# Re-ordering a one-core layer kernel: a scheduler with measured durations, weight norms on other engines, and one row sent ahead

## The chip, the cores and the metric

The kernel runs on one core of a Trainium2 chip. The metric is the device time of one execution in microseconds (us); the medians below come from three to seven executions. The executions of this study were spread over several chips, so a kernel is compared with the kernel before of the same call wherever that can be done. A ratio is the mean time of one kernel's fast runs over that of the other's fast runs in the same rounds, so it is not quite the ratio of the medians quoted. For one core, a run is called slow when it lies over 1.5% above the fastest run of the same kernel. A "pause" of PE is the time from the start of one matmul to the start of the next, less the time that such a matmul usually takes (0.216 us for 512 columns).

Names: PE is TensorE, PEld its weight loads, DVE is VectorE, ACT is ScalarE, POOL is GpSimd, SP is SyncE, which issues most transfers.

## The reference, cut to what matters

```python
def _A_ref(x, wqkv, w_phi, wo):        # H = 32 heads of 16
    ...                                # q, k, v = x @ wqkv
    phi_q = concat(softmax(q @ w_phi), softmax(-(q @ w_phi)));  phi_k likewise
    kv = phi_k^T v;  z = sum(phi_k);  o = (phi_q kv) / (phi_q z + 1e-6)
    return o @ wo
def _B_ref(x, w_gate, w_up, w_down):   # D = 512, F = 1792
    return ((x @ w_gate) * (x @ w_up)) @ w_down
xn = layernorm(x)                      # 2048 tokens x 512
return x + _A_ref(xn, ...) + _B_ref(xn, ...)
```

## The kernel before

The program is a list of steps, each with an engine, its reads and its writes. A scheduler written in Python turns the list into one fixed order per engine before the kernel is built; semaphores are then placed from the reads and writes. The order on PE is given by the program ("pinned"); the other engines' orders come from the scheduler's model of time. On the chip each engine runs its list strictly in order (below, DVE stands 4.58 us before one instruction while the next ones wait).

The main loop walks 19 slots `t`. A slot does the k features of token tile `t`, two or three "up units" (gate and up matmuls of 128 rows of F for 512 tokens, then a gate multiply on DVE that frees their PSUM banks, the `ps` tiles that matmuls write), v, from slot 8 on q features, and pieces of side work: norms of the weights (to choose power-of-two scales for half precision), scaling of the weights by DVE, sums and differences of weight blocks ("combinations", used for a multiplication with seven instead of eight products), and, for the first 512 tokens, whose inputs were centred but not divided by their standard deviation, a multiply of h by a row of r2 = 1/variance ("normalise", on POOL).

```python
def row_of_r2():                       # slot 10: after the scale sh of h is known
    pool(lambda e: e.tensor_scalar(out=r2s, in0=r2, scalar1=sh, ...), ["r2", "sh"], ["r2s"], 4)
    row = nc.dram_tensor("r2row", (ND, 128), F32, kind="Internal").ap()
    o = row.rearrange("t p -> p t")    # 128 partitions x 4 values: 512 writes of 4 bytes
    sc.dma(SP, lambda e: e.dma_start(o, r2s, allow_slow_non_contiguous=True), ["r2s"], ["r2row"], 131072)
    ...                                # read back, spread over all partitions
    sc.dma(SP, lambda e: e.dma_start(r2w, wide), ["r2row"], ["r2w"] + ks, 262144, free=ks)

def scales(t):                         # side work of slot t
    if t in (9, 10):   ...             # squares of wv, wo on ACT
    if 2 <= t < 9:                     # squares of w_gate and w_up on ACT, one each per slot
        squares("wg", t - 2, last); squares("wu", t - 2, last)
    elif t == 10:
        h_scale(); row_of_r2()
    if 7 <= t < 10:    wd_moments(...)     # 14 bn_stats of w_down on DVE
    if t == 11:        d_scale()
    if 12 <= t < 15:   scale_weights(todo[3 * (t - 12):3 * (t - 11)], last)
    elif t == 16:      combine_weights(1); combine_weights(2)
    elif t == 17:      combine_weights(3)
    ...
# in slot t:
    if 10 <= t < NT + 1:
        normalise(range(2 * (t - 10), 2 * (t - 9)), [("hT", *latest[0])])

def _order(sc):                        # the scheduler
    LAT, DMA_ISSUE, DMA_FIXED, TURN_ISSUE = 200.0, 550.0, 1700.0, 1300.0
    ...                                # of the ready steps of an engine, that with the best
                                       # priority among those that can start within 100 ns
```

Of the kernel before, what the change touches and what calls it, by code (L numbers as in the profile page):

```python
# [125 lines left out]
def _build(nc, es, A_x, A_wqkv, A_w_phi, A_wo, B_w_gate, B_w_up, B_w_down, out):  # L126
# [246 lines left out]
    def w_fold(w, dt, b=None):  # L373
        b = misc_bank() if b is None else b

        def fn(e):
            ins = None
            for jt in range(NQ):
                ins = e.matmul(bank(b, jt * 128, 128), lhsT=wT_v[:, w, jt, dt * 128:(dt + 1) * 128],  # L379
                               rhs=wbd_v[:, jt, :], start=True, stop=True)  # L380
            return ins
        sc.step(PE, fn, [("wT", w, jt) for jt in range(NQ)] + [("wbd", jt) for jt in range(NQ)], [("ps", b)], 4 * 60.0)
        if w == 1 or dt % 2 == 0:
            act(Wp_v[:, w, dt, :], bank(b), [("ps", b)], [("Wp", w, dt)])
        else:
            dve(lambda e: e.tensor_copy(out=Wp_v[:, w, dt, :], in_=bank(b)), [("ps", b)], [("Wp", w, dt)], 512)
# [264 lines left out]
    def squares(src, i, after):  # L651
        j = squared[0] % 4
        squared[0] += 1
        junk = hT_v[:, NF - 8 + 2 * j:NF - 6 + 2 * j, 3 * 512:4 * 512]
        over = [("junk", j)] if squared[0] > 4 else []
        if src in ("wv", "wo"):
            v, col, key = (wv_v, 14 + i, [("wv", i)]) if src == "wv" else (wo_v, 16 + i, ["wo"])
            act(junk, v[:, 2 * i:2 * i + 2, :], key + after + over, [("junk", j), ("ssq", col)], func=ACTF.Square,
                accum=ssq[:, col:col + 1])
        else:  # L660
            v, col = (wg_v, i) if src == "wg" else (wu_v, 7 + i)
            i_ap = v[:, :, i * 256:(i + 1) * 256].rearrange("p (a b) c -> p a b c", a=2)
            key = [(src, k) for k, (lo, n) in enumerate(SLICES) if lo < (i + 1) * 256 and lo + n > i * 256]
            act(junk.rearrange("p a (b c) -> p a b c", b=2), i_ap, key + after + over, [("junk", j), ("ssq", col)],
                func=ACTF.Square, accum=ssq[:, col:col + 1])
# [4 lines left out]
    def wd_moments(fts, after):  # L670
        sc.prio = 2
        for ft in fts:
            dve(lambda e, ft=ft: e.bn_stats(wst[:, ft, :], wd_v[:, ft, :]), ["wd"] + after, [("wst", ft)], 512)  # L673
        sc.prio = 1
        if fts[-1] == NF - 1:
            dve(lambda e: e.bn_aggr(wmv, sbf("wst", 0, NF * 6)), [("wst", ft) for ft in range(NF)], ["wmv"], 84)
            dve(lambda e: e.scalar_tensor_tensor(out=wmv[:, 0:1], in0=wmv[:, 0:1], scalar=wmv[:, 0:1], in1=wmv[:, 1:2],
                                                 op0=ALU.mult, op1=ALU.add), ["wmv"], ["wms"], 1)
            dve(lambda e: e.tensor_scalar(out=ssq[:, 18:19], in0=wmv[:, 0:1], scalar1=NF * 512.0, scalar2=None,
                                          op0=ALU.mult), ["wms"], [("ssq", 18)], 1)  # L680
# [11 lines left out]

    def norms(lo, groups, c0):
        n, k = sum(groups), len(groups)
        cols = [("ssq", c) for c in range(lo, lo + n)]
        dve(lambda e: e.tensor_copy(out=ssqb[:, lo:lo + n], in_=ssq[:, lo:lo + n]), cols, [("ssqb", lo)], n)
        b = misc_bank()
        mm(bank(b, 0, n), [(nc.const_aps.tensor(1.0, (128, 128), BF16), ssqb[:, lo:lo + n])], [("ssqb", lo)], b)
        for i, m in enumerate(groups):
            at = sum(groups[:i])  # L700
            dve(lambda e, i=i, m=m, at=at: e.tensor_reduce(out=scl[:, c0 + i:c0 + i + 1], in_=bank(b, at, m),
                                                           axis=AX.X, op=ALU.add), [("ps", b)], [("nrm", lo, i)], m)
        act(scl[:, c0 + 4:c0 + 4 + k], scl[:, c0:c0 + k], [("nrm", lo, i) for i in range(k)] + ["eps"], [("lnn", lo)],
            func=ACTF.Ln, bias=tiny)
        act(scl[:, c0 + 8:c0 + 8 + k], scl[:, c0 + 4:c0 + 4 + k], [("lnn", lo)], [("rn", lo)], func=ACTF.Exp,
            scale=-0.5)

    def h_scale():
        norms(0, (7, 7), 8)
        dve(lambda e: e.tensor_tensor(out=scl[:, 20:21], in0=scl[:, 16:17], in1=scl[:, 17:18], op=ALU.mult),  # L710
            [("rn", 0)], ["rgu"], 1)
        power_of_two(sh, scl[:, 20:21], ["rgu"], "sh", 8.0)


    def d_scale():
        norms(14, (2, 2, 1), 24)
# [29 lines left out]
    def row_of_r2():  # L746
        pool(lambda e: e.tensor_scalar(out=r2s, in0=r2, scalar1=sh, scalar2=None, op0=ALU.mult), ["r2", "sh"], ["r2s"],
             4)
        row = nc.dram_tensor("r2row", (ND, 128), F32, kind="Internal").ap()
        o = row.rearrange("t p -> p t")  # L750
        sc.dma(SP, lambda e: e.dma_start(o, r2s, allow_slow_non_contiguous=True), ["r2s"], ["r2row"], 131072)
        ks = [("x", 12), ("x", 13)]
        wide = bass.AP(tensor=row.tensor, offset=row.offset, ap=[[0, 128], [1, ND * 128]])
        sc.dma(SP, lambda e: e.dma_start(r2w, wide), ["r2row"], ["r2w"] + ks, 262144, free=ks)

    def normalise(fts, after):
        sc.prio = 2
        for ft in fts:
            pool(lambda e, ft=ft: e.tensor_tensor(out=hH_v[:, ft, 0:512], in0=hT_v[:, ft, 0:512], in1=r2w,  # L759
                                                  op=ALU.mult), [("hT", ft, 0), "r2w", ("x", 12), ("x", 13)] + after,  # L760
                 [("hT", ft, 0)], 512)
        sc.prio = 1

    r2s = scl[:, 4:4 + ND]
    r2w = sbf("x", 3072, 512)
# [12 lines left out]
    def combine_weights(k):  # L778
# [3 lines left out]
        for name, t, blk, n, src, ov in (("tw", tw, wd_block, NK, [("wdh", i) for i in range(7)], over),  # L782
                                         ("two", two, wo_block, 2, [("woh", i) for i in range(2)], ov_o)):
            i0, i1 = {1: (blk(0, 1), blk(0, 0)), 2: (blk(1, 1), t[1]), 3: (blk(1, 1), blk(0, 1)),
# [58 lines left out]
    glu = [0]  # L843
    raw = set()
# [24 lines left out]
    def gate(ft, sg, bg, bu, s):  # L869
        g = sb("g", s * 512, 512)  # L870
        if "sh" not in sc.writer:
# [180 lines left out]
    def scales(t):  # L1052
        last = [("hT", *latest[0])] if latest[0] else []
        if t in (9, 10):
            for i in range(2):
                squares("wv" if t == 9 else "wo", i, last)
        if 2 <= t < 9:
            squares("wg", t - 2, last)
            squares("wu", t - 2, last)
        elif t == 10:  # L1060
            h_scale()
            row_of_r2()
        if 7 <= t < 10:
            wd_moments(((0, 1, 2, 3, 4, 5), (6, 7, 8, 9), (10, 11, 12, 13))[t - 7], last)
        if t == 11:
            d_scale()
        if 12 <= t < 15:
            scale_weights(todo[3 * (t - 12):3 * (t - 11)], last)
        elif t == 16:
            combine_weights(1)  # L1070
            combine_weights(2)
        elif t == 17:
            combine_weights(3)
        if t == 11:
            halves.extend([to_half(1), to_half(2)])
        if t >= 11:
            half_step(1)
# [26 lines left out]
    for t in range(NT + 3):  # L1104
# [9 lines left out]
        x_next(t + 4)  # L1114
        late_loads(t)
# [6 lines left out]
        if 12 <= t < NT + 1:  # L1122
            if t not in (14, 16):
                up()
            if t in (13, 15):
                q_next()
# [5 lines left out]
        else:  # L1132
            up()
            if 8 <= t < NT + 1:
                q_next()
            if 10 <= t < NT + 1:
                normalise(range(2 * (t - 10), 2 * (t - 9)), [("hT", *latest[0])])
            if 3 <= t < NT + 2:
                kv_acc(t - 3)
            if t < 12 and t != 10:  # L1140
                up()
        if 4 < t < 8:
            w_fold(0, (0, 1, 3)[t - 5])
    h_combine(0)
# [32 lines left out]

def _order(sc):


    LAT, DMA_ISSUE, DMA_FIXED, TURN_ISSUE = 200.0, 550.0, 1700.0, 1300.0
    dma_free = 0.0
    steps = sc.steps
    remaining = [len(st.deps) for st in steps]
# [11 lines left out]
    free_at = {e: 0.0 for e in ready}  # L1196
    new_order = {e: [] for e in ready}
    order = []
    while len(order) < len(steps):
        best = None  # L1200
        for e, lst in ready.items():
            if pos[e] < len(fixed[e]):
                lst = [p for p in lst if not steps[p[1]].pin or p[1] == fixed[e][pos[e]]]
            if lst:
                fa = free_at[e]
                soon = min(max(p[0], fa) for p in lst) + 100.0
                cand = min((p for p in lst if p[0] <= soon), key=lambda p: (steps[p[1]].prio, max(p[0], fa), p[1]))
                key = (max(cand[0], fa), cand[1])
# [7 lines left out]
        if isinstance(st.lane, tuple):  # L1216
            issue = TURN_ISSUE if st.turn else DMA_ISSUE
            free_at[e] = start + issue
            dma_free = max(dma_free, start + issue) + st.cost
            st.finish = dma_free + DMA_FIXED  # L1220
        else:
            free_at[e] = start + st.cost
            st.finish = free_at[e]
# [3 lines left out]
        for d in dependents[idx]:  # L1227
            remaining[d.idx] -= 1
            ready_time[d.idx] = max(ready_time[d.idx], st.finish + (LAT if d.lane != st.lane else 50.0))
# [86 lines left out]
```

## Time and profile before

| | before |
|---|---|
| time, three runs | 215.57, 215.76, 216.53 us |
| the run that was profiled | 219.02 us, span 217.3 us |
| PE busy | 96% |
| matmul pauses from 108 to 141 us | 4.0 us |

The page of the kernel before, busy time of the engines and two rows of the 40 slices (each digit is a tenth of a slice of 5.4 us):

```profile
PE 209.5 (96%) x1476; PEld 124.9 (57%) x1476; DVE 174.4 (80%) x279; ACT 145.2 (67%) x349; POOL 114.3 (53%) x138
PE   7899999999999999999999998699999999999995
PEclk9999999999999999999999999999999999999999
PE 80%; DVE 12%; issue 3%; DMA 3%; ACT 1%; SPq 0%
```

The last line is the chain of work that ended last, by engine: mostly PE, with DVE for 12%. The "86" in the PE row, at 130 to 141 us, is where PE was short of work. The list of waits of PE names the releaser (engine, tile, line; then total us, times, longest us):

```profile
PE ps L247 <- DVE arena L878: 3.0, 3, 1.7
PE ps L985 <- PEq L1301: 0.8, 1, 0.8
```

L878 is the gate multiply on DVE. In the same trace the groups of DVE instructions by shape (busy us, mean ns) and two transfers in the list of DMAs (KB each, median us from issue to landing) read:

```profile
L733 DVE TENSOR_SCALAR arena<-arena 128x1024 f16<-128x1024 bf16 x9 | 7.8, 899 | 0.1
L787 DVE TENSOR_TENSOR arena<-arena 128x1792 f16<-128x1792 f16 x4 | 7.7, 1914 | 0.0
arena<-in_A_x_dram SPq DMA_DIRECT2D x3, 512.0 KB, 4.3
r2row<-arena SPq DMA_DIRECT2D x1, 2.0 KB, 8.2
```

Weight scaling (L733) and combinations (L787) are the DVE instructions that meet POOL at the port the two share.

### The profile page before, as it was taken

What the parts mean: (1) busy time and instruction counts of PE and PEld (TensorE: products, weight loads), DVE (VectorE), ACT (ScalarE), POOL (GpSimd) and SP (SyncE); (2) the same over time, 40 slices, a digit from 0 to 9 for tenths busy, and PEclk for the clock granted to TensorE, in tenths of its full rate; (3) what the DMA queues carried; (4) which work ended last, traced back from release to release, by engine and by line L of the source; (5) the groups of instructions that cost most, each with busy time, mean ns of one, the idle gap of its engine ahead of it and who ended that gap; (6) DMA issues with size and microseconds to landing.
All of it is one profiled execution on the core that took longest, in us unless ns stands there. A gap on an engine that the chain in (4) does not pass through costs nothing.

```text
span 217.3 us, 4042 instructions
## 1 busy us (share of the span) xinstructions
PE 209.5 (96%) x1476; PEld 124.9 (57%) x1476; DVE 174.4 (80%) x279; ACT 145.2 (67%) x349; POOL 114.3 (53%) x138
## 2 busy tenths in 40 slices
PE   7899999999999999999999998699999999999995
PEld 2574444444554444444444443245898898899884
DVE  3838989966499896769699999996998898898722
ACT  5588899887887898996859587486535435432220
POOL 4032454440332155241999998831858568568540
PEclk9999999999999999999999999999999999999999
DMA  5999871892000021205202520552329547547411
GB/s 174 287 293 370 167 167 32 270 280 49 0 3 0 0 48 27 27 3 97 51 0 48 97 51 0 101 141 48 51 67 153 127 96 171 121 100 172 121 48 48
DMA packets 49075, 22.29 MB, mean 103 GB/s; under 512 B 38048, under 2 KB 47392, under 8 KB 49056
## 3 DMA queue, kind: packets, MB, share of 16 engines
q1 hardware_dynamic: 48112, 21.39, 42.0%
q10 hardware_dynamic: 944, 0.66, 1.0%
q14 instruction: 8, 0.07, 0.4%
q8 instruction: 11, 0.18, 0.4%
HBM read 11.03 MB, written 2.10 MB: 60 GB/s over the span
## 4 chain that ended last, share of the span: by engine, by line
PE 80%; DVE 12%; issue 3%; DMA 3%; ACT 1%; SPq 0%
PE ps L247 76%; DVE arena L787 4%; DVE arena L518 4%; DMA arena<-in_A_wqkv_dram 3%; DVE arena L878 2%; DVE arena L733 2%; PE ps L622 2%; PE ps L564 1%; PE ps L379 1%; ACT arena L228 1%; SPq L272 0%; DVE arena L908 0%; PE ps L486 0%
## 5 line engine op out<-in xcount | busy, mean ns | idle before, releaser
L247 PE MATMUL ps<-arena 128*128 128x512 bf16 (+2 forms) x1160 | 200.7, 330 | 3.9 <-DVE arena L878 3.0
L247 PEld LDWEIGHTS ps<-arena 128*128 128x128 bf16 (+1 forms) x1160 | 110.3, 98 | 78.5 <-DVE arena L878 4.8
L228 ACT ACTIVATE arena<-ps 128x512 bf16<-128x512 f32 (+4 forms) x119 | 60.3, 537 | 18.9 <-PE ps L247 14.7
L228 ACT ACTIVATE arena<-arena 128x32 f32<-128x32 f32 (+8 forms) x132 | 54.1, 423 | 11.9 <-DVE arena L518 8.1
L878 DVE TENSOR_TENSOR arena<-ps,arena 128x512 bf16<-128x512 f32 (+1 forms) x56 | 37.9, 683 | 13.0 <-PE ps L247 8.6
L528 POOL TENSOR_TENSOR arena<-arena 128x1024 bf16<-128x1024 bf16 x16 | 31.8, 1990 | 24.4 <-ACT arena L228 24.4
L518 DVE TENSOR_REDUCE arena<-arena 128x64 f32<-128x1024 bf16 x32 | 38.6, 1214 | 4.7 <-ACT arena L228 4.5
L228 ACT ACTIVATE arena<-ps,arena 128x512 bf16<-128x512 f32 (+1 forms) x51 | 32.4, 650 | 7.3 <-PE ps L247 7.1
L840 POOL TENSOR_TENSOR arena<-arena 128x256 f16<-128x256 f16 x32 | 24.3, 769 | 9.1 <-DMA arena<-arena 7.8
L818 DVE TENSOR_TENSOR arena<-arena 128x896 f16<-128x896 f16 x32 | 26.7, 836 | 2.7 <-PE ps L247 2.4
L228 ACT ACTIVATE ps<-ps 128x256 f32<-128x256 f32 x24 | 8.8, 368 | 29.0 <-PE ps L247 29.0
L759 POOL TENSOR_TENSOR arena<-arena 128x512 f16<-128x512 bf16 x14 | 19.3, 1393 | 9.1 <-DMA arena<-r2row 7.3
L908 DVE SCALAR_TENSOR_TENSOR arena<-ps,arena 128x256 bf16<-128x256 f32 (+1 forms) x24 | 13.2, 565 | 8.7 <-PE ps L247 8.5
L943 POOL TENSOR_TENSOR arena<-arena 128x512 f32<-128x512 f32 x8 | 9.7, 1213 | 16.7 <-ACT arena L228 16.7
L534 POOL TENSOR_TENSOR arena<-arena 128x512 bf16<-128x512 bf16 x16 | 17.1, 1070 | 1.3
L632 DVE TENSOR_TENSOR arena<-ps,arena 128x512 f16<-128x512 f32 x16 | 10.9, 684 | 1.3 <-ACT arena L228 0.5
L532 POOL TENSOR_TENSOR arena<-arena 128x32 f32<-128x32 f32 x16 | 5.3, 331 | 12.4 <-ACT arena L228 12.4
L787 DVE TENSOR_TENSOR arena<-arena 128x1792 f16<-128x1792 f16 (+1 forms) x8 | 11.6, 1464 | 0.1
L406 DVE BATCH_NORM_STATS2 arena<-arena 128x6 f32<-128x512 bf16 x16 | 10.5, 667 | 0.0
L464 POOL TENSOR_SCALAR arena<-arena 128x1 f32<-128x1 f32 x12 | 3.2, 286 | 13.6 <-ACT arena L228 13.6
L673 DVE BATCH_NORM_STATS2 arena<-arena 128x6 f32<-128x512 bf16 x14 | 8.6, 681 | 0.2
L564 PEld LDWEIGHTS ps<-arena 128*128 128x128 bf16 x128 | 6.0, 97 | 3.5
(57 smaller groups left out, 71.6 us busy)
## 6 DMA issues: line engine op xcount, KB each, us to landing
arena<-in_A_x_dram SPq DMA_DIRECT2D x9, 256.0 KB, 3.2
out_dram<-arena SPq DMA_DIRECT2D x15, 128.0 KB, 2.0
arena<-in_B_w_down_dram SPq DMA_DIRECT2D x1, 1792.0 KB, 8.4
arena<-in_A_x_dram SPq DMA_DIRECT2D x3, 512.0 KB, 4.3
arena<-arena SPq DMA_TRANSPOSE x44, 3.1
arena<-in_B_w_gate_dram SPq DMA_DIRECT2D x1, 640.0 KB, 8.7
arena<-in_B_w_up_dram SPq DMA_DIRECT2D x1, 640.0 KB, 9.9
arena<-in_B_w_gate_dram SPq DMA_DIRECT2D x1, 512.0 KB, 5.2
```

The lines of the kernel that those rows point to most:

```text
L228: return sc.step(ACT, lambda e: e.activation(out=out_ap, in_=in_ap, func=func, scale=scale, **kw), reads, writes, 130.0 + 0.833 * n)
L247: ins = e.matmul(out_ap, lhsT=l, rhs=r, start=start and i == 0, stop=stop and i == npair - 1, **kw)
L518: dve(lambda e: e.tensor_reduce(out=sm, in_=e_v, axis=AX.X, op=ALU.add), [(name, s, 0), (name, s, 1)], [("sums", sr)], 1024)
L528: pool(lambda e: e.tensor_tensor(out=e_w, in0=e_w, in1=r_w, op=ALU.mult), [(name, s, 0), (name, s, 1), ("rs", n)], [(name, s, 0), (name, s ...
L534: pool(lambda e: e.tensor_tensor(out=e_v[:, :, 1, :], in0=e_v[:, :, 1, :], in1=rat[:, :, None].to_broadcast([128, H, 16]), op=ALU.mult), [ ...
L632: dve(lambda e: e.tensor_tensor(out=o_tile(t).rearrange("p (b h f) -> p b h f", b=2, f=16), in0=nd[:, :, :, 0:16], in1=w_v[:, r].unsqueeze ...
L759: pool(lambda e, ft=ft: e.tensor_tensor(out=hH_v[:, ft, 0:512], in0=hT_v[:, ft, 0:512], in1=r2w, op=ALU.mult), [("hT", ft, 0), "r2w", ("x" ...
L787: dve(lambda e, o=t[k], i0=i0, i1=i1: e.tensor_tensor(out=o, in0=i0, in1=i1, op=ALU.subtract), src + need, [(name, k)] + ov, n * 256, 0.52)
L818: dve(lambda e, k=k, i0=i0, i1=i1, op=op: e.tensor_tensor(out=s_block(p, k), in0=i0, in1=i1, op=op), ks + more, [s_key(p, k)] + over.get(k ...
L840: pool(lambda e, k=k, i0=i0, i1=i1, op=op: e.tensor_tensor(out=so_block(p, k), in0=i0, in1=i1, op=op), ks + [("so", p, m) for m in more], ...
L878: dve(lambda e: e.tensor_tensor(out=h_v[:, ft, sg * 512:(sg + 1) * 512], in0=bank(bu), in1=g, op=ALU.mult), [("ps", bu), ("g", s)] + ([("j ...
L908: dve(lambda e: e.scalar_tensor_tensor(out=o, in0=src, scalar=inv, in1=resid, op0=ALU.mult, op1=ALU.add), keys + [rkey, "inv"], [("ostg", ...
```

## The change

Its intent: take side work out of the stretch where DVE is full. The row of r2 is written to memory early and unscaled, so normalise can start in slot 9 instead of slot 10 plus a wait; w_up is measured by bn_stats on DVE in slots 5 and 6 and w_down by squares on ACT, so that the scale of h is known in slot 8; weight work moves forward and spreads; and the scheduler gets durations close to measured ones, a model of the shared port, and a first-in first-out model of DMA.

```diff
     def row_of_r2():
-        pool(... r2s = r2 * sh ...)
         row = nc.dram_tensor("r2row", (ND, 128), F32, kind="Internal").ap()
         o = row.rearrange("t p -> p t")
-        sc.dma(SP, lambda e: e.dma_start(o, r2s, allow_slow_non_contiguous=True), ["r2s"], ["r2row"], 131072)
+        sc.dma(SP, lambda e: e.dma_start(o, r2, allow_slow_non_contiguous=True), ["r2"], ["r2row"], 1500000)
+    def wide_row(): ...      # reads it back, slot 6
+    def scale_row():         # times sh, on ACT, slot 8
+        act(r2w, r2w, ["r2x", "sh", ...], ["r2w"], func=ACTF.Identity, scale=sh)
 ...
     def scales(t):
+        for src, i in {6: [("wv", 0), ("wv", 1)], 7: [("wd", 0), ("wd", 1), ("wd", 2)],
+                       8: [("wd", 3), ("wd", 4), ("wd", 5)], 9: [("wd", 6), ("wo", 0), ("wo", 1)]}.get(t, ()):
+            squares(src, i, last)
+        if t in (5, 6):
+            moments(range(7 * (t - 5), 7 * (t - 4)), last)      # bn_stats of w_up
+        if t == 8:  norms(0, (7, 1), 8); h_scale(); scale_row()
+        if t == 4:  row_of_r2()
+        elif t == 6: wide_row()
+        if 11 <= t < 14:  scale_weights(...)                    # was 12 to 14
+        ... combinations in slots 14, 15, 16, 17                # were 16, 17
 ...
-            if 10 <= t < NT + 1:
-                normalise(range(2 * (t - 10), 2 * (t - 9)), ...)
+            if 9 <= t < 14:
+                normalise(range(3 * (t - 9), min(NF, 3 * (t - 8))), ...)
-            if t in (13, 15): q_next()
+            if t in (9, 11, 13): q_next()
 ...
 def _order(sc):
-    LAT, DMA_ISSUE, DMA_FIXED, TURN_ISSUE = 200.0, 550.0, 1700.0, 1300.0
+    SEM, SAME, TURN, ISSUE, LANDS = 60.0, 30.0, 1280.0, 350.0, 1500.0
+    ...                      # _cost(st): length per step and whether it holds the port; lock_free
```

Two evictions also move from DVE to ACT, and some priorities change. Matmuls stay the same but for the widths of the two tiny norm matmuls.

## The prediction

> **What bounds the kernel now.** TensorE: 96% busy on the page. The timeline's start-to-start times say more: 216 ns per 512-column matmul, 109 ns per 256. All 1476 matmuls at such paces make 205.9 us of the 217.3 us span. The chain of waits runs through PE from 7.5 to 108.5 us and from 141.5 us to the last store; only from 108.5 to 141.5 us does it run through VectorE. There the matmul stream pauses four times (114.4, 130.9, 136.7, 140.8 us): 0.44 + 1.23 + 1.82 + 0.48 = 4.0 us; the list of waits puts 3.0 us of PE's idle time on the gate multiplies of VectorE. The rest is head (slow clock, first x tile, about 3 us) and tail (3 us after the last matmul); the change barely touches either.
>
> **Why VectorE is late there.** The windows view shows it 9.0 to 10.0 us busy of each 10 from 110 to 150 us. The same instruction varies with POOL beside it: weight scaling (1024 columns) takes 0.48 to 1.39 us, the 1792-column weight combinations 1.07 to 2.70, the 512-column ones 0.42 to 1.38. Against their shortest times these 17 lose about 9 us. The Trainium skill ("SBUF — State Buffer", section "Who interferes with whom") calls the port pair of GpSimd and VectorE an exclusive lock, for VectorE instructions in two-port modes or with two SBUF inputs; these durations agree. POOL is full there because all 14 normalise multiplies (1.39 us each, 19.3 us) wait for the row of r2, which lands at 102 us: POOL idles 7.3 us for that DMA.
>
> **What the change does.**
> - The row leaves unscaled in slot 4, returns in slot 6 and is scaled on ScalarE (about 0.7 us). Normalise can start near 72 us, three per slot in slots 9 to 13: about 15 us of POOL work leaves the stretch.
> - w_up is measured by 14 bn_stats (0.68 us) in slots 5 and 6, where VectorE has room (5.4 to 7.3 of 10 us); w_down goes to ScalarE, 7 squares (1.04 + 0.19 us) in place of w_up's 7. Counts are equal, but the h scale is known two slots earlier, and two of nine conversions to half fall away.
> - Weight scaling moves one slot earlier; the combinations spread over slots 14 to 17, after normalise.
> - Two evictions (0.68 us) move from VectorE to ScalarE.
> - Matmuls keep their count and nearly their order; 52 up units precede the output stages in both.
> - The scheduler orders by lengths nearer those measured and knows the lock.
>
> **How much is critical.** At most the 4.0 us of pauses. VectorE should gain some 7 us of slack in the stretch, so they should nearly vanish. Against it: ScalarE is near 90% busy from 70 to 100 us, and slots 8 and 9 get three squares each, slot 9 a second q tile too. By the start-to-start times it just fits, but I expect 0.5 to 1 us of new pauses around the two norm matmuls or the gates after them. Net gain 3 us.
>
> **Predicted: 212.7 us, 80% range 211.0 to 214.8. Faster by over 2%: 0.13; within 2%: 0.84; slower by over 2%: 0.03.**
>
> **What would show it.** Right: PE pauses from 108 to 141 us under 1 us; the chain runs through PE almost throughout; normalise lies in about 72 to 115 us; the 1792-column combinations average nearer 1.2 than 1.9 us. Wrong: pauses in the stretch with combinations still 2 us long, or new pauses over 1 us at slots 8 to 11, released by ScalarE.
>
> **What would make it wrong.** Low: the new order also shortens head or tail. High: combinations still meet POOL's k and q multiplies, or ScalarE's backlog of squares holds up a norm matmul, whose place in PE's order is fixed.

## More of the kernel before

The layer norm moments of a token tile are one step on DVE that reads the tile as soon as it is loaded:

```python
def ln_moments(t):
    dve(lambda e: e.bn_stats(stats_v[:, t, 0:6], x_tile(t)), [("x", t)], [("st", t)], 512)
    ...
```

## The result, and the profile after

The kernel after took 223.5 us (median of four: 223.46, 223.81, 223.54, 221.90), against 215.94 us before in the same rounds; ratio 1.0333, interval 1.0277 to 1.0388. It is slower by 3.3%, where I had forecast 1.4% faster.

The same lines of the page after (slices of 5.5 us):

```profile
PE 212.4 (96%) x1476; PEld 125.4 (57%) x1476; DVE 171.0 (77%) x277; ACT 144.8 (65%) x350; POOL 109.8 (49%) x137
PE   8899939999999899999999999999999999999995
PEclk9999985999999999999999999999999999999999
PE 69%; DMA 11%; DVE 7%; SPq 6%; ACT 4%; issue 1%; DVEq 0%
PE ps L247 <- DVE arena L902: 3.6, 1, 3.6
PE ps L247 <- ACT arena L228: 0.9, 1, 0.9
```

The hole in the stretch from 108 to 141 us is gone: after 77 us every slice of PE but the last reads 9. There is a new hole in the sixth slice, at 28.9 us, and right behind it the granted clock falls ("85" in the PEclk row). The chain now has more of transfers (11% instead of 3%) and 6% of SP's queue. The waits of PE (last two lines) are one of 3.6 us for a gate multiply, L902, and one of 0.9 us for ACT.

What DVE did around the hole, before and after, in order of time (start, us, operation, and in brackets its idle time with the releaser):

```profile
24.75 0.68 DVE L878 TENSOR_TENSOR arena<-ps,arena 128x512 bf16<-128x512 f32 x1
25.35 0.68 DVE L406 BATCH_NORM_STATS2 arena<-arena 128x6 f32<-128x512 bf16 x1
26.05 1.22 DVE L518 TENSOR_REDUCE arena<-arena 128x64 f32<-128x1024 bf16 x1
27.19 0.68 DVE L878 TENSOR_TENSOR arena<-ps,arena 128x512 bf16<-128x512 f32 x1
```

```profile
25.12 0.68 DVE L902 TENSOR_TENSOR arena<-ps,arena 128x512 bf16<-128x512 f32 x1
30.38 0.69 DVE L403 BATCH_NORM_STATS2 arena<-arena 128x6 f32<-128x512 bf16 x1 [4.58 <-DMA arena<-in_A_x_dram]
30.99 1.20 DVE L515 TENSOR_REDUCE arena<-arena 128x64 f32<-128x1024 bf16 x1
32.10 1.28 DVE L902 TENSOR_TENSOR arena<-ps,arena 128x512 bf16<-128x512 f32 x2
```

The order is the same in both: gate, bn_stats of x tile 8, reduce, gate. Before, tile 8 is there at 25.35 us. After, DVE stands for 4.58 us in front of bn_stats, because the load of x has not landed, and the gates behind it wait too. PE then runs out of PSUM banks:

```profile
25.64 3.62 PE L247 MATMUL ps<-arena 128*128 128x512 bf16 x16
32.84 7.52 PE L247 MATMUL ps<-arena 128*128 128x512 bf16 x21 [3.58 <-DVE arena L902]
```

In the second line 21 matmuls take 7.5 us: for 12 of them the start-to-start time is about 0.427 us instead of 0.216 us (two more take 0.40 and 0.33 us). The trace's clock record has half the clock from 31.75 to 38.58 us, 6.83 us in all. The Trainium skill ("TensorE: Matmul & The Clock Gate", section "What's actually happening") says that the array is slowed to half after an idle window and that the window is 3413 ns long and free-running; two such windows are 6.83 us, so this trace agrees on the length. It does not agree that the window must be idle throughout: in the one before the drop, 28.34 to 31.75 us, PE still worked for its first 0.75 us.

The traces with a clock record, taken together, show what matters. Cut into windows of 3.41 us that end where the clock changes, with PE counted as working for 0.216 us from each start of a matmul of 512 columns, the five windows after which the clock fell have 2.18 to 3.41 us of idle PE (row_late_old_order, stats_held, after, before_dummy_row, after_again), and no window after which it stayed full has more than 2.14 us. So a pause costs a window of half clock if enough of it falls into one window, and the same pause cut in two by a window's end may not.

The same two lines of the list of DMAs after:

```profile
arena<-in_A_x_dram SPq DMA_DIRECT2D x3, 512.0 KB, 10.0
r2row<-arena SPq DMA_DIRECT2D x1, 2.0 KB, 16.1
```

The load of x tiles 8 to 11 was issued at 14.2 us and landed 16.1 us later; before it took 10.4 us. The row of r2 was issued right behind it, at 15.7 us. "Slot 4" in the program had not meant slot 4 in time: the step depends on r2 alone, which POOL has ready at 13.8 us, and the scheduler put it as early as it could.

The sum, from the start-to-start times of the matmuls: the four pauses in the stretch are gone (-4.0 us); the pause at 28.9 us costs 3.75 us, the half clock 2.8 us, the first norm matmul at 76.5 us 1.06 us, three small pauses at 62 to 68 us 0.45 us, and the head 0.4 us. That makes +4.5 us, as do the spans (217.26 and 221.73 us). This is against the profiled run of before, at 219.02 us. The other 3 us of the measured difference lie between that run and the timed ones of before, of which no trace exists (experiments 7 and 9).

### The profile page after: what moved, and what is told of

Its sections match the earlier page's. It is cut to its first block, busy times and chain, and to the rows that moved or that the text cites. A ratio compares the mean times of both kernels' runs of the same rounds, so it can differ in the third digit from the quotient of the medians.

```text
span 221.7 us, 4044 instructions
## 1 busy us (share of the span) xinstructions
PE 212.4 (96%) x1476; PEld 125.4 (57%) x1476; DVE 171.0 (77%) x277; ACT 144.8 (65%) x350; POOL 109.8 (49%) x137
## 4 chain that ended last, share of the span: by engine, by line
PE 69%; DMA 11%; DVE 7%; SPq 6%; ACT 4%; issue 1%; DVEq 0%
PE ps L247 66%; DMA arena<-in_A_x_dram 7%; ACT arena L228 4%; DMA arena<-arena 4%; SPq L296 3%; DVE arena L676 2%; SPq L292 2%; DVE arena L515 2%; PE ps L619 2%; PE ps L561 1%; DVE arena L902 1%; SPq L272 1%; DVE arena L463 1%; DVE arena L403 0%; DVE arena L932 0%
## 5 line engine op out<-in xcount | busy, mean ns | idle before, releaser
L247 PE MATMUL ps<-arena 128*128 128x512 bf16 (+2 forms) x1160 | 203.5, 333 | 4.7 <-DVE arena L902 3.6
L228 ACT ACTIVATE arena<-ps 128x512 bf16<-128x512 f32 (+4 forms) x117 | 58.9, 540 | 13.1 <-PE ps L247 7.5
L228 ACT ACTIVATE arena<-arena 128x32 f32<-128x32 f32 (+9 forms) x131 | 52.9, 420 | 18.1 <-DVE arena L515 13.5
L902 DVE TENSOR_TENSOR arena<-ps,arena 128x512 f16<-128x512 f32 (+1 forms) x56 | 38.3, 685 | 15.6 <-ACT arena L228 8.4
L228 ACT ACTIVATE arena<-ps,arena 128x512 bf16<-128x512 f32 (+1 forms) x55 | 35.2, 661 | 11.6 <-PE ps L247 11.4
L841 DVE TENSOR_TENSOR arena<-arena 128x896 f16<-128x896 f16 x32 | 26.0, 812 | 3.0 <-PE ps L247 3.0
L781 POOL TENSOR_TENSOR arena<-arena 128x512 f16<-128x512 bf16 x14 | 16.3, 1174 | 6.4 <-DVE arena L902 4.2
L403 DVE BATCH_NORM_STATS2 arena<-arena 128x6 f32<-128x512 bf16 x16 | 10.4, 670 | 4.6 <-DMA arena<-in_A_x_dram 4.6
L463 DVE TENSOR_SCALAR arena<-arena 128x512 bf16<-128x512 bf16 x12 | 5.4, 485 | 2.5 <-DMA arena<-arena 2.5
```

Of the source, the lines that this page charges most:

```text
L228: return sc.step(ACT, lambda e: e.activation(out=out_ap, in_=in_ap, func=func, scale=scale, **kw), reads, writes, 130.0 + 0.833 * n)
L247: ins = e.matmul(out_ap, lhsT=l, rhs=r, start=start and i == 0, stop=stop and i == npair - 1, **kw)
L781: pool(lambda e, ft=ft: e.tensor_tensor(out=hH_v[:, ft, 0:512], in0=hT_v[:, ft, 0:512], in1=r2w, op=ALU.mult), [("hT", ft, 0), "r2w", ("x" ...
L841: dve(lambda e, k=k, i0=i0, i1=i1, op=op: e.tensor_tensor(out=s_block(p, k), in0=i0, in1=i1, op=op), ks + more, [s_key(p, k)] + over.get(k ...
L902: dve(lambda e: e.tensor_tensor(out=h_v[:, ft, sg * 512:(sg + 1) * 512], in0=bank(bu), in1=g, op=ALU.mult), [("ps", bu), ("g", s)] + ([("j ...
```

## The experiments

Eighteen runs were made, of sixteen new kernels and two repeats. "Before" in a result is the kernel before of the same call. It took 218.2 to 219.3 us in all these, not 215.6 to 216.5 as in the first runs; experiments 7 and 9 are about that.

**1. row_late: the row sent later.** The kernel after, with its row behind the transpose of tile 10.

```diff
-        if t == 4:
+        if t == 6:
             row_of_r2()
-        elif t == 6:
+        elif t == 7:
             wide_row()
-        ... ["r2"], ["r2row"], 1500000)
+        ... ["r2", ("xnT", 10)], ["r2row"], 1500000)
```

> Kernel after, with the one scattered write of the row of r2 (4-byte packets) put behind the transpose of tile 10 in the DMA queue (about 45 to 50 us instead of 15.7 us), its read back one slot later; the order of the instructions on VectorE at 25 us stays: bn_stats of x tile 8 ahead of the next gates. Theory A (the early row delays the landing of x tiles 8 to 11, and VectorE waits for them in order): landing of that load falls from 16 us to about 10 us, the 3.7 us pause of TensorE at 28.9 us and the half clock after it vanish, time 212 to 214 us. Theory B (the new scheduler's order on VectorE is at fault whatever the row does): the pause stays and the time stays at 222 to 224 us.

Measured: 215.99 us (215.46 to 216.54), ratio 0.9873 to a before of 218.86. The row is issued at 49.9 us; the x load lands in 10.3 us; DVE's order is the same and nothing waits:

```profile
24.13 0.68 DVE L902 TENSOR_TENSOR arena<-ps,arena 128x512 bf16<-128x512 f32 x1
24.73 0.68 DVE L403 BATCH_NORM_STATS2 arena<-arena 128x6 f32<-128x512 bf16 x1
25.44 1.22 DVE L515 TENSOR_REDUCE arena<-arena 128x64 f32<-128x1024 bf16 x1
```

The clock is full throughout. Theory A holds and B falls. The time is above the 212 to 214 us of the expectation; the gain over the before of the same chip, 2.8 us, is close to the 3 us predicted.

**2. before_dummy_row: the same row, alone, in the kernel before.**

```diff
+    def early_row():
+        dummy = nc.dram_tensor("r2dummy", (ND, 128), F32, kind="Internal").ap()
+        o = dummy.rearrange("t p -> p t")
+        sc.dma(SP, lambda e: e.dma_start(o, r2, allow_slow_non_contiguous=True), ["r2"], ["r2dummy"], 131072)
     def scales(t):
+        if t == 4: early_row()
```

> Kernel before, with one more scattered write of r2 (2 KB in 4-byte packets, to a tensor that nobody reads), issued where the kernel after issues its row. Theory A: the load of x tiles 8 to 11 lands about 5 us later, bn_stats holds up VectorE, TensorE pauses 3 to 4 us near 29 us and then runs at half clock; time 221 to 225 us. Theory B: no effect beyond 0.5 us, 215.5 to 216.5 us.

Measured: 221.51 and 224.56 us in the two fast runs (225.27 and 227.60 in the slow ones), ratio 1.0194 (interval 1.0109 to 1.028, so slower, but unclear whether by 2%). The profiled run is a slow one, but the fast ones are longer than before as well, by 2.7 and 5.7 us. In the trace the x load lands after 17.1 us and PE pauses 4.66 us at 28.4 us, with half the clock behind it (the list of transfers of x, of which the longest is this load, and the waits of PE):

```profile
DMA to landing us min/median/max: 2.6/3.2/17.1
PE ps L248 <- DVE arena L879: 7.5, 4, 4.5
```

So the idle row alone makes the late landing, the pause and the half clock, in a kernel that has nothing else of the change.

**3. before_dummy_16b: the same bytes in fewer pieces.** The dummy tensor is laid out `(128, ND)`, so each partition writes 16 contiguous bytes.

> As before_dummy_row, but the extra write is contiguous per partition: 128 packets of 16 bytes instead of 512 of 4 bytes, at the same place in the queue. If the number of tiny writes costs the time (theory A, form 1), the landing of x tiles 8 to 11 slips by 2 us or less and TensorE pauses under 1 us: within 1 us of before. If any write to memory in that place waits that long (form 2), the pause is again 3 to 5 us.

Measured: 215.52, 215.63, 218.45 and (slow) 218.87 us, ratio 0.9914. The x load lands in 10.4 us and PE does not pause near 29 us:

```profile
DMA to landing us min/median/max: 2.6/3.2/10.4
```

So the number of tiny writes matters (or their size, which changed with it), not a write in that place. That it came out faster than before was not expected; experiments 7 and 9 come back to it.

The packets by microsecond of start, from the trace's packet records, say what the 512 tiny writes do:

```
            before_dummy_16b                     before_dummy_row
22 to 23    16 B x80 mean 9 ns, ...              4 B x324 mean 9 ns, 256 B x394 mean 20 ns
25 to 26    4096 B x26 mean 533 ns               4096 B x15 mean 4361 ns
26 to 27    4096 B x79 mean 175 ns               none
27 to 28    4096 B x20 mean 159 ns, ...          4096 B x12 mean 1007 ns
```

The tiny packets themselves are short. So are those of the load that lands late: x tiles 8 to 11 are 128 packets of 4096 bytes, and in before_dummy_row these start at 20.5 us and are over by 23.7 us, as in before_dummy_16b. What is late is the report: a load reports its landing in 16 parts, and here eight of them come by 22.5 us, the other eight from 24.25 to 30.75 us (the last one in before_dummy_16b at 24.27 us). The slow packets in the table belong to the next load, of tiles 12 to 15, issued at 23.8 us: for about 6 us they take 0.6 to 4.4 us on average instead of mostly 0.16 to 0.18 us.

The row's own report takes as long even where no load is near: in the kernel before the packets of the row start at 90.1 us and are over by 90.5 us, and its 16 reports come from 95.7 to 97.4 us; in row_late they are over by 51.2 us, and the reports come from 56.3 to 58.1 us. So sending the row later does not shorten it; it puts the wait where no engine needs a load. The traces do not show what is waited for in that time.

**4. row_act_queue: the early row on another queue.** One word of the kernel after: `sc.dma(SP,` becomes `sc.dma(ACT,` for the row.

> The kernel after with one word changed: its early row of r2 is issued from ScalarE's DMA queue instead of SyncE's, at the same time (about 16 us). If the load of x tiles 8 to 11 is late because it stands in the same queue as the tiny writes, it lands in about 10 us again, TensorE does not pause near 29 us, and the time is that of row_late (215.5 to 217 us). If the tiny writes hold up the 16 engines that both queues share, the landing slips to 15 to 17 us, the pause of 3 to 5 us stays and the time is 218.5 to 224 us, as in after_again.

Measured: 219.28, 220.89, 222.53 and (slow) 224.25 us, ratio 1.0105. The x load lands after 16.1 us, and PE pauses 3.9 us at 28.0 us:

```profile
PE ps L247 <- DVE arena L902: 3.7, 1, 3.7
```

So standing in the same queue is not the reason: SP's queue is held up by a row from another one. Here the packets of the x load themselves are slow (20.5 to 29.2 us). The Trainium skill ("DMA: Bandwidth & Descriptors", section "Issuing engines are not separate DMA queues") says that queues issued from different engines run on the same 16 DMA engines; this run agrees. In the profiled run the clock stayed full in spite of 3.9 us of pause (a window ends at 30.25 us and cuts it into 2.04 and 1.86 us); the other runs had mean clocks of 0.992, 0.992 and 0.985, which fits one, one and two windows of 3.4 us at half clock in 217 to 222 us. So kernels with the early row scatter over 5 to 6 us.

**5. after_again: the kernel after on a chip with a before of 218.8 us.** No edit.

> The kernel after, unchanged, timed on the chip of this call, since the kernel before took 215.9 us on one chip and 218.9 us on another. If the loss is the same everywhere, 3 to 4% over the before of this call; its pause near 29 us should again be 3 to 5 us, with one or two windows of half clock behind it.

Measured: 218.59 us once (fast, clock 1.0) and 222.66, 223.44, 224.60 us (called slow for it, clocks 0.985 to 0.992). The trace has the same hole, 4.61 us at 28.3 us, and a landing of 17.0 us.

**6. stats_held: early row, but no bn_stats ahead of the gates.**

```diff
     def ln_moments(t):
-        ... [("x", t)], [("st", t)], 512)
+        held = [("hT", *latest[0])] if t >= 8 else []
+        ... [("x", t)] + held, [("st", t)], 512)
```

> Kernel after, row still early, but the bn_stats of x tiles 8 to 15 are made to wait for a later gate multiply, so that none of them can stand ahead of the gates while its tile has not landed. Theory A: the load still lands at about 30 us, but TensorE does not pause at 29 us; 212 to 215 us. If the late DMA stops TensorE by another way (weights, transposed tiles), the pause stays and so do 222 to 224 us.

Measured: 217.09, 217.49, 220.17 and (slow) 220.71 us, ratio 0.9976. The landing is still late (16.4 us), yet DVE goes on and PE has no pause near 29 us:

```profile
24.86 0.68 DVE L903 TENSOR_TENSOR arena<-ps,arena 128x512 bf16<-128x512 f32 x1
26.17 1.22 DVE L516 TENSOR_REDUCE arena<-arena 128x64 f32<-128x1024 bf16 x1 [0.62 <-ACT arena L228]
27.30 0.68 DVE L903 TENSOR_TENSOR arena<-ps,arena 128x512 bf16<-128x512 f32 x1
```

So the late landing makes that pause only because bn_stats stands ahead of the gates in a fixed order. The expected 212 to 215 us did not come: in the trace of the slow run PE pauses 2.85 us at 90.3 us at the second norm matmul, for a DVE cast that the new order had put behind two reduces; that pause, too, is followed by a window of half clock.

**7. Why before has two times.** Experiment 3 has exactly the order of before on every engine, plus one write at 15 us, and yet ran at 215.5 or 218.5 us. Its short, profiled run has 0.8 us of pauses in the stretch; the profiled run of before has 4.0 us. Set side by side, they part where the row of r2 arrives: POOL's first normalise starts 0.35 us later against DVE's work in the short run. Six us later both want the port at the same time. Before, POOL comes first (first two lines); in the short run, DVE does:

```profile
109.04 3.78 POOL L759 TENSOR_TENSOR arena<-arena 128x512 f16<-128x512 bf16 x3
109.22 3.88 DVE L733 TENSOR_SCALAR arena<-arena 128x1024 f16<-128x1024 bf16 x3
120.66 2.70 DVE L787 TENSOR_TENSOR arena<-arena 128x1792 f16<-128x1792 f16 x1
```

```profile
109.00 3.09 DVE L734 TENSOR_SCALAR arena<-arena 128x1024 f16<-128x1024 bf16 x3
109.17 3.95 POOL L760 TENSOR_TENSOR arena<-arena 128x512 f16<-128x512 bf16 x3
119.41 1.09 DVE L788 TENSOR_TENSOR arena<-arena 128x1792 f16<-128x1792 f16 x1
```

The three scalings take 3.09 instead of 3.88 us (the first 0.49 instead of 1.27 us, the others 1.38 us in both), and at 120 us the first combination takes 1.09 instead of 2.70 us, since it now starts ahead of POOL's next multiply. The exclusive lock of the port pair that the prediction quoted from the Trainium skill fits: of two that meet, one runs at its own length and the other waits (the first scaling 0.49 us in the short run, POOL's first multiply 1.17 us before). That the order at 109 us is what makes the run short or long is a reading of these two traces, not yet a test.

**8. before_vector_first: an edit that did not act.** The normalise multiplies of slots 12, 13, 14 and 16 were made to wait for weight work of their slot, by adding its keys to their reads.

> The kernel before took 215.6 to 216.5 us in some runs and 218.3 to 219.3 us in others, and one more idle write (before_dummy_16b) switched it between 215.5 and 218.9 us with the same order of instructions, the pauses from 108 to 141 us being 0.8 us in the short one and 4.0 us in the long one. Theory: who takes the shared port first at about 109 us (a weight scaling of VectorE or a normalise multiply of POOL, 0.1 to 0.2 us apart) decides it. Here the normalise multiplies of slots 12, 13, 14 and 16 wait for VectorE's weight work of their slot, so VectorE goes first always. If the theory holds, all runs lie at 215 to 216.5 us and the pauses there are under 1.2 us. If it falls, the time follows the before of this call.

Measured: 218.88 us, ratio 1.0016, and the same four pauses (0.44, 1.23, 1.81, 0.48 us). In the trace POOL still comes first, at 108.71 us against DVE's 108.88: the multiply there belongs to a slot whose added wait was long over. The run tells nothing of the race.

**9. before_pool_nudge: 0.2 us more work.** One idle POOL instruction between the landing of the row and the first normalise; the orders of the other engines are unchanged.

```diff
         sc.dma(SP, lambda e: e.dma_start(r2w, wide), ["r2row"], ["r2raw"] + ks, 262144, free=ks)
+        pool(lambda e: e.tensor_scalar(out=nudge, in0=r2w[:, 0:1], scalar1=1.0, scalar2=None, op0=ALU.mult),
+             ["r2raw"], ["r2w"], 1)
```

> The kernel before, with one idle POOL instruction (about 0.3 us) between the landing of the row of r2 and the first normalise multiply; all other orders are the same. Set side by side, the long run of before and the short run of before_dummy_16b part at 102.3 us, where the row lands 0.33 us later against VectorE, and at 109 us, where VectorE then gets the port ahead of POOL (0.49 instead of 1.27 us for one weight scaling). If this race makes the two modes, 0.3 us of more work makes the kernel faster: 215.3 to 216.5 us in all runs against a before at 218.5 to 219, with pauses under 1.2 us from 108 to 141 us. If not, it stays at the before of this call.

Measured: 215.26, 215.58 and 215.79 us, ratio 0.9851 to a before of 218.9; and one slow run, the profiled one, at 220.62 us. The instruction took 0.23 us. In the slow run POOL's first normalise starts only 0.20 us later against DVE than in before, instead of 0.35; DVE and POOL then start within 0.02 us of each other and DVE's scaling is held up all the same:

```profile
110.60 2.78 DVE L733 TENSOR_SCALAR arena<-arena 128x1024 f16<-128x1024 bf16 x2
110.62 2.47 POOL L762 TENSOR_TENSOR arena<-arena 128x512 f16<-128x512 bf16 x2
```

Its pauses are again 0.64, 1.23, 1.82 and 0.48 us (the rest of its length is a slower head). So an added instruction makes before 3.3 us faster in three of four runs. This supports the race; the short runs of it have no trace, and of the first runs of before at 215.6 to 216.5 us none has one either, so that those were the short mode is inferred from their times. Before itself took 218.2 to 219.3 us in all 35 later runs, on four chips, and the shorter times in its first runs alone; that the chip of those runs had a part in it is not excluded.

**10. before_new_order: the new scheduler alone.** The function `_order` and its cost model from after, everything else from before.

> The kernel before with the new scheduler alone (measured lengths, port lock, DMA model); every step and every slot as before, the row of r2 late as before. If the scheduler carries the gain, the four pauses from 108 to 141 us shrink to 1 to 2 us together and the time falls by 2 to 3 us. If the moved normalise multiplies carry it, VectorE stays full there, the pauses stay near 4 us and the time within 1 us of before.

Measured: 218.67 us, ratio 0.9984. Pauses in the stretch remain in other places (1.92, 0.54, 0.27 us from 116 to 124 us, 0.66 us at 151 us). Alone it gains nothing against the long mode.

**11. row_late_old_order: row_late with the scheduler of before.**

> As row_late, but with the scheduler of the kernel before. Tells what the new scheduler is worth. If the gain in the stretch 108 to 141 us comes from moving the normalise multiplies and spreading the combinations, this is within 1 us of row_late (213 to 214 us) and its pauses there are under 1 us. If it comes from ordering by measured lengths and the port lock, the 4 us of pauses come back: 216 us or more.

Measured: 220.99 us, ratio 1.0098: 5 us over row_late. The pauses in the stretch are small (0.41 and 0.70 us), but ACT holds PE up for 2.18 us at 100.2 us, and three of four runs have a window of half clock. With the old scheduler the steps of the change bring a loss; 2.18 us of pause was enough for the clock to fall.

**12. row_late_norm_old: normalise back in slots 10 to 16.** The diff of the normalise lines above, reversed, in row_late.

> As row_late, with the normalise multiplies back in slots 10 to 16, two per slot. If moving them carries the gain in the stretch 108 to 141 us, pauses of 2 to 4 us come back there and the time rises 2 to 4 us over row_late_again. If the scheduler carries it, the time stays within 1 us.

Measured: 215.90 us, ratio 0.9873; **row_late_again**, the same kernel as row_late on the same chip, 216.03 us, ratio 0.9882.

> row_late unchanged, on the chip of this call, for comparison with the three others and with a before that may be in its short or its long mode: 215.3 to 216.6 us again, 1.3% below a before in its long mode and level with one in its short mode.

No pause came back in the stretch, although POOL is 8 to 10 of 10 us busy from 120 to 140 us again. The step that I had named as the main gain is worth nothing here, as long as the rest of row_late is there.

**13. The other moved steps.** In row_late: weight work back in its old slots; q tiles back in their old slots; and normalise, weight work and q tiles all back.

> As row_late, with the weight scaling and the combinations back in the slots of before (12 to 14; 16 and 17). row_late_norm_old showed that the moved normalise multiplies are worth nothing. If the moved weight work carries the gain, pauses of 1.5 to 4 us come back between 110 and 150 us, and the time is 217 to 219.5 us. If not, within 1 us of row_late (216.0).

> As row_late, with the q tiles back in the slots of before (the second ones in slots 13 and 15, the last in 16), so two more q tiles, with their 1.2 us reduces, fall in the full stretch. If that carries the gain, pauses of 1.5 to 4 us come back between 110 and 145 us and the time is 217 to 219.5 us. If not, within 1 us of row_late (216.0).

> As row_late, with normalise, weight work and q tiles all in the slots of before; what stays of the change is the scheduler, the swap of bn_stats and squares, the earlier h scale and the row sent ahead. If the moves to other slots carry the gain only together, 217.5 to 219.5 us. If the rest carries it, within 1 us of row_late.

Measured: 216.11, 216.35 and 216.44 us (ratios 0.9874, 0.9876 and 0.9913). No pause over 0.4 us is left in the stretch in any. What these kernels still share with row_late is the new scheduler, the swap of squares and bn_stats, the earlier scale, and the row of r2 that is there before it is needed, so that normalise no longer starts when a transfer happens to land. Which of these keeps the pauses away was not taken apart further.

**14. The pause at the first norm matmul.** In row_late PE waits 0.9 us for ACT there:

```profile
PE ps L247 <- ACT arena L228: 0.9, 1, 0.9
```

row_late_spread takes the squares of w_down apart, two per slot with one of wo left in slot 10; row_late_spread2 moves those of wv to slot 5 and those of w_down to slots 6, 7, 8 and 9 as 2, 3, 1 and 1; row_late_best adds the old q slots to the latter.

```diff
-{6: [("wv", 0), ("wv", 1)], 7: [("wd", 0), ("wd", 1), ("wd", 2)], 8: [("wd", 3), ("wd", 4), ("wd", 5)], 9: [...]}
+{5: [("wv", 0), ("wv", 1)], 6: [("wd", 0), ("wd", 1)], 7: [("wd", 2), ("wd", 3), ("wd", 4)], 8: [("wd", 5)], 9: [...]}
```

> As row_late, with the squares of w_down, two per slot from slot 6 on instead of three in slots 7 and 8, so that ScalarE frees the PSUM bank that the first norm matmul waits for. If ScalarE's backlog of squares makes the 1.07 us pause at the norm matmul (67 us in row_late), it shrinks under 0.4 us and the time is 0.5 to 1 us below row_late, some 1.7% below before. If not, the pause stays.

> As row_late, with the squares of wv moved ahead to slot 5 and those of w_down to slots 6, 7 and 8 as 2, 3 and 1 (row_late_spread put one into slot 10, and the second norm matmul waited 2.2 us for it). If ScalarE's squares near the norm matmuls make the pauses, the 1.07 us one of row_late shrinks under 0.4 us, none appears at the second, and the time is 0.5 to 1 us below row_late_again. If the pauses only move about with the order, no gain.

> row_late_spread2 with the q tiles of the slots of before (in row_late_q_old the pause at the first norm matmul was 0.71 instead of 1.07 us). If both shorten that pause, it falls under 0.3 us and the time is 214.8 to 215.4 us, 0.2 to 0.6 us under row_late_spread2 (215.6) and under the short mode of before (215.5 to 216.5). If the order reshuffles, 215.5 to 216.5 us.

Measured: row_late_spread 218.83 us (ratio 1.0005), a miss: PE pauses 2.23 us at the second norm matmul and 2.0 us in three pieces at 55 to 61 us. row_late_spread2 215.57 us (215.37 to 216.09, ratio 0.9859): the pause shrinks from 1.07 to 0.40 us, and PE's wait for ACT in its list to

```profile
PE ps L247 <- ACT arena L228: 0.2, 1, 0.2
```

row_late_best 215.61 us (215.00 to 216.35, ratio 0.9856), no better. These two are clearly below the kernel after, and 1.4% below before in its long mode; they are level with before in its short mode and with before plus the idle instruction of experiment 9.

## Why the prediction was wrong

- **Right: the pauses in the stretch go away.** From 108 to 141 us the kernel after has none over 0.1 us (predicted under 1 us). The 1792-column combinations average 1.18 us (predicted nearer 1.2 than 1.9). A pause of 0.5 to 1 us at the norm matmuls was predicted; it was 1.06 us.
- **Wrong, the step that failed: "The row leaves unscaled in slot 4".** I listed this as a saving and gave the transfer no cost, nor a wait for anything that it might delay. The scheduler issues it at 15.7 us, between the loads of x, and its 512 writes of 4 bytes delay the landing of x tiles 8 to 11 from 10.4 to 16.1 us after their issue. DVE's fixed order turns that into 3.75 us of pause and the half clock adds 2.8 us: 6.6 us in place of the zero that I had put down. Shown by row_late (take it away: 216.0 us), before_dummy_row (add it alone: +2.7 and +5.7 us in fast runs), before_dummy_16b (same bytes in 128 writes: no such pause) and row_act_queue (other queue: no help). Two signs were in the profile before: 2 KB that took 8.2 us, and a load that landed at 24.3 us for a bn_stats that began at 25.35 us, a margin of 1 us on an engine that cannot step around it.
- **Wrong: the base.** I subtracted pauses seen in a run of 219.02 us from a time of 215.76 us, and made no use of the difference of 3.3 us. The four pauses were seen only in runs of before and its variants of 218 us and more; which of the two times comes seems to depend on who takes the shared port first. An idle instruction of 0.23 us made three of four runs 3.3 us shorter, which supports this and does not prove it. From 219.0 the predicted 3 us lead to 216.0, which is what row_late measured; since the reason given for these 3 us was wrong (next point), this agreement is luck. A kernel that already runs at 215.8 has little of this left to gain. So the early row is not the whole error: row_late too lies above the range of the prediction.
- **Wrong: the reason given for the gain.** Moving the normalise multiplies out of the stretch is worth nothing by itself (row_late_norm_old, 215.90 against 216.03 us). That the lock of the port lengthens DVE's instructions there was right, but less work on POOL in the stretch was not needed to take away the pauses.
- **Open:** what is waited for after the tiny writes; whether the shared port alone makes the two times of before; and which of the parts shared by row_late_all_old and row_late removes the pauses.

## What to carry to other kernels

Before moving a transfer earlier, look at how long it takes to land and at what else is in flight at its new place: count its packets, not its bytes, and check when it will be issued, since a step with few dependencies goes out far ahead of the slot in which it is written. In a fixed order, an instruction that waits for a transfer must not stand ahead of those that free what TensorE needs, and a pause of 2.2 us or more may cost up to nearly twice its length, because the clock can drop behind it (3.75 + 2.8 us here); it also may not. When the profiled run and the timed runs differ by more than the change is expected to bring, find out why before predicting: here both times were of the same program, and the longer one, in the profile, showed a gain that the other did not have.

## What the Trainium skill lacked or had wrong

- "DMA: Bandwidth & Descriptors", section "Why small descriptors are slow (HBM only)": it gives costs per packet, which do not tell this effect. Here 512 writes of 4 bytes took 9 ns each, but the last report of a load whose packets were already over came at 30.75 instead of 24.27 us, and for about 6 us the 4096-byte packets of the next load took 0.6 to 4.4 us on average instead of mostly 0.16 to 0.18 us; a row from another queue held up the load as well (landing after 16.1 us). 128 writes of 16 bytes had no such effect (landing after 10.4 us). The page's section "Anatomy of one DMA — SWDGE (gpsimd) path" says that a transfer's report waits until its last byte has landed in memory; no page says that many tiny writes stretch this to 5 to 7 us (row_late), or that other transfers of the same core wait with them.
- "SBUF — State Buffer", section "Who interferes with whom": it says that issue order decides who blocks, and two traces agree (a weight scaling takes 0.49 us where it starts first and 1.27 us where it starts second, at the same place). In the slow run of before_pool_nudge the scaling started 0.02 us first and still took 1.47 us, so starts that close do not tell the order. It lacks how far this may reach: with 0.35 us of shift in one start, a kernel with the same orders took 215.5 instead of 219.0 us.
- "TensorE: Matmul & The Clock Gate", section "What's actually happening": the window and the half clock agree (6.83 us for two, 0.427 us per 512 columns), but the clock fell after windows with 2.18 us of idle PE out of 3.41, not only after idle ones. It lacks how much of a window must be idle: here 2.14 us or less never cost the clock, and a pause of 3.9 us that a window's end cut in two did not either (row_act_queue: 219.3 us with none, 224.3 us with a mean clock of 0.985).
